# Moving part of a feed-forward stage between the attention batches of a routed kernel

## The chip, the cores and the metric

The kernel runs on one core of a Trainium2 chip. The metric is the device time of one execution in microseconds (us), as the median of several runs. The engines are named as in the profile: PE (TensorE, matmuls), PEld (its weight loads), DVE (VectorE), ACT (ScalarE), POOL (GpSimd) and SP (SyncE, which issues transfers).

## The reference, cut to what matters

```python
# q, k, v: batch 8, heads 8, sequence 576, head size 64
scores = scale * q @ k.T;  mask = |i - j| <= 32
x = softmax(scores) @ v                        # laid out as 4608 rows of 512
logits = x @ w_gate + modality_bias[modality]  # 8 experts
e_idx = argmax(logits);  gate_w = softmax(logits)[e_idx]
for e in range(8):                             # rows of expert e only
    out[mask] = gate_w * (relu(x[mask] @ w1[e]) @ w2[e])   # 512 -> 1024 -> 512
```

With the fixed inputs only two experts are used: expert 0 by 2300 rows and expert 4 by 2308.

## The kernel before

The kernel works through eight batches. Each has **attention** (transpose queries and keys, scores, Exp, mask, product with the values) and then **routing** (transpose the rows, logits, the expert of each row, the row's rank within its expert, and a scatter of the rows to a scratch in HBM, grouped by expert). When all batches are done it makes a table of 256-row tiles on the chip and runs the **feed-forward** tile by tile. PSUM is the memory into which PE writes here, and which DVE or ACT then read. Each stage has its own PSUM buffers, since a stage's pools are closed before the next stage opens its own. "tag" and "bufs" say which tiles share a buffer and how many there are.

```python
# attention and routing
ps_s bufs=1, ps_o bufs=1, ps_t bufs=2                # PSUM pools of this stage
for b in range(B):
    ...
    for hp in range(H // 2):                         # a pair of heads
        for u in range(2):
            tp = ps_t.tile([P, R, P], BF16, tag="tp")
            ...                                      # 4 transposes, then a copy to qkT
        sA = ps_s.tile([P, 2, 512], FP32, tag="sA")  # two score buffers
        sB = ps_s.tile([P, 2, 512], FP32, tag="sB")
        ...
        oA = ps_o.tile([P, 3, 2, D + 1], FP32, tag="oA")
        oB = ps_o.tile([P, 2, 2, D + 1], FP32, tag="oB")
        ...
    lg = ps_o.tile([P, NM, E], FP32, tag="oB")       # logits: an output buffer
    for m in range(NM):
        tp = ps_t.tile([P, n_kd, P], BF16, tag="tp")
        ...                                          # transpose, copy, 4 matmuls into lg
    ...
    rk = ps_o.tile([P, NM + 1, E], FP32, tag="oA")   # ranks: an output buffer
    ...                                              # 5 scatters to scr
# feed-forward, with pools of its own
fps_t bufs=2, fps_h bufs=3, fps_y bufs=3
def ffn(tiles, pools, first_block):
    ...
    for x_ in range(n):
        i = tiles[x_]
        if x_ + 1 < n:
            stage_load(tiles[x_ + 1])                # fetched and transposed a tile ahead
        up(i)                                        # 32 matmuls, Relu on ACT
        if x_:
            down(tiles[x_ - 1])                      # 16 matmuls, gate on DVE, scatter on POOL
    down(tiles[-1])
```

The softmax here doesn't subtract the row's maximum and nothing guards it: scores larger than these inputs give would overflow.

Of the kernel before, what the change touches and what calls it, by code (L numbers as in the profile page):

```python
# [31 lines left out]
def kernel(  # L32
# [28 lines left out]
    NTILE = N // TT + E - 1  # L61
    NK = N // TT
    BIG = 65536.0
    n_kd = HD // P
# [4 lines left out]
    wpool = ctx.enter_context(tc.tile_pool(name="wpool", bufs=1))  # L69
    small = ctx.enter_context(tc.tile_pool(name="small", bufs=2))  # L70

    scr = dram.tile([E * N, ROW // 2], I32)


    ident = const.tile([P, P], BF16)
    make_identity(nc, ident[:])

# [6 lines left out]
    nc.gpsimd.memset(mask[:], 1.0)  # L84
    for j in range(2):
# [6 lines left out]
    nc.gpsimd.memset(maskl[:], 1.0)  # L92
    m_ap = maskl[:]
    nc.gpsimd.affine_select(out=m_ap, in_=m_ap, compare_op=ALU.is_ge, fill=0.0,
                            base=64, pattern=[[1, 96]], channel_multiplier=-1)
    nc.gpsimd.affine_select(out=m_ap, in_=m_ap, compare_op=ALU.is_ge, fill=0.0,
                            base=0, pattern=[[-1, 96]], channel_multiplier=1)
    nc.gpsimd.affine_select(out=m_ap, in_=m_ap, compare_op=ALU.is_ge, fill=0.0,
                            base=-64, pattern=[[0, 96]], channel_multiplier=1)
# [8 lines left out]
    def iota_f(shape, pattern, base, cm):  # L108
        n = 1
        for s_ in shape[1:]:  # L110
            n *= s_
        ti = const.tile([P, n], I32, name=f"ioi{iota_f.c}")
        tf = const.tile([P, n], FP32, name=f"iof{iota_f.c}")
        iota_f.c += 1
        nc.gpsimd.iota(ti[:], pattern=pattern, base=base, channel_multiplier=cm)
        nc.vector.tensor_copy(tf[:], ti[:])
        return ti, tf
    iota_f.c = 0
    ids_i, _ = iota_f([P, B, NM], [[S, B], [P, NM]], -32, 1)
    _, io_e8 = iota_f([P, E], [[1, E]], -E, 0)  # L120
    _, io_row = iota_f([P, E], [[N, E]], 0, 0)
    _, io_k = iota_f([P, NK], [[TT, NK]], 0, 0)
    _, io_p2 = iota_f([P, 2], [[P, 2]], 0, 1)
    _, io_t = iota_f([P, NTILE], [[1, NTILE]], 0, 0)

# [4 lines left out]
    le = const.tile([P, E, E], FP32)  # L130
    nc.gpsimd.memset(le[:], 1.0)
    nc.gpsimd.affine_select(out=le[:], in_=le[:], compare_op=ALU.is_ge, fill=0.0,
                            base=0, pattern=[[1, E], [-1, E]], channel_multiplier=0)

    sgn = const.tile([P, NTILE + 1], FP32)
    nc.gpsimd.memset(sgn[:], 0.0)
    nc.gpsimd.memset(sgn[:].rearrange("p (n two) -> p n two", two=2)[:, :, 0:1], 1.0)
    off = const.tile([P, NTILE + 1], FP32)
    off_i = const.tile([P, NTILE + 1], I32)
    nh = (NTILE + 1) // 2  # L140
    nc.gpsimd.iota(off_i[:, 0:nh], pattern=[[-1, nh]], base=-1, channel_multiplier=0)
    nc.gpsimd.iota(off_i[:, nh:2 * nh], pattern=[[1, nh]], base=0, channel_multiplier=0)
    nc.vector.tensor_copy(off[:].rearrange("p (n two) -> p two n", two=2),
                          off_i[:].rearrange("p (two n) -> p two n", two=2))
# [4 lines left out]
    nc.scalar.dma_start(mb_bc[:], moe_modality_bias.partition_broadcast(P))  # L149
# [4 lines left out]
    for m in range(NM):  # L154
        p0 = 32 if m == 0 else 0
        p1 = 96 if m == NM - 1 else P
        s0 = P * m - 32
        nc.scalar.dma_start(mid64[B * m:B * m + B, p0:p1], idv[:, s0 + p0:s0 + p1])
# [4 lines left out]
    with (tc.tile_pool(name="setup", bufs=1) as sup,  # L163
          tc.tile_pool(name="setup_ps", bufs=1, space=bass.MemoryType.PSUM) as sup_ps):
        midp = sup_ps.tile([P, NM * B], BF16)
        nc.tensor.transpose(midp[:], midr[:], ident[0:NM * B, 0:NM * B])
        msel = sup.tile([P, NM * B], FP32)
        mtmp = sup.tile([P, NM * B, E], FP32)
        for m_ in range(n_mod):
            nc.vector.tensor_scalar(out=msel[:], in0=midp[:], scalar1=float(m_), scalar2=None,  # L170
                                    op0=ALU.is_equal)
            dst = bias if m_ == 0 else mtmp
            nc.vector.tensor_tensor(
                out=dst[:], in0=msel[:].unsqueeze(2).to_broadcast([P, NM * B, E]),
                in1=mb_bc[:, m_, :].unsqueeze(1).to_broadcast([P, NM * B, E]), op=ALU.mult)
            if m_:
                nc.vector.tensor_tensor(out=bias[:], in0=bias[:], in1=mtmp[:], op=ALU.add)
    bias_v = bias[:].rearrange("p (m b) e -> p m b e", b=B)

    w1_sb = [wpool.tile([P, n_kd, F], BF16, name=f"w1_{i}") for i in range(2)]  # L180
    w2_sb = [wpool.tile([P, n_kf, HD], BF16, name=f"w2_{i}") for i in range(2)]
# [10 lines left out]
    def reg(ap, engines, lo, hi):  # L192
        return nc.values_load(ap, engines=engines, min_val=lo, max_val=hi,
                              skip_runtime_bounds_check_because="the table is clamped on chip")



    qk_t = [const.tile([P, H // 2, 2, 32 + S], BF16, name=f"qkT{i}") for i in range(2)]
    p_t = [const.tile([P, 2, PW], BF16, name=f"pt{i}") for i in range(3)]
    v_t = [const.tile([P, NM, H, D + 1], BF16, name=f"vt{i}") for i in range(2)]  # L200
    x_t = [const.tile([P, NM, ROW // 2], I32, name=f"xt{i}") for i in range(2)]
    for t_ in x_t:
        nc.gpsimd.memset(t_[:, :, HD // 2 + 2:ROW // 2], 0)
    for t_ in qk_t:
        nc.gpsimd.memset(t_[:, :, 0, 0:32], 0.0)
    for t_ in p_t:
        nc.gpsimd.memset(t_[:, :, 0:4 * SW].rearrange("p h (j c) -> p h j c", c=SW)[:, :, :, WIN:SW], 0.0)
        nc.gpsimd.memset(t_[:, :, 4 * SW + WL:PW], 1.0)
    for t_ in v_t:
        nc.gpsimd.memset(t_[:, :, :, D:D + 1], 1.0)  # L210
        nc.gpsimd.memset(t_[0:P - SR, NM - 1, :, 0:D], 0.0)

    zero = const.tile([P, TT // P, ROW // 2], I32)
    nc.gpsimd.memset(zero[:], 0)

    zero_ins, scr_ins = [], []

    def after(ins, others):
        for o_ in others:
            tc.add_manual_dep(ins.ins, o_.ins.name, mybir.DependencyInfo(  # L220
                mybir.DependencyClass.Sync, mybir.DependencyReason.DATA), reason="scratch rows")

    def unordered(ins, group):

        tc.declare_no_dep(ins.ins, group=group, reason="disjoint rows")
        tc.add_to_no_dep_group(group, ins.ins)

    base = const.tile([P, E], FP32)
    ext_e = const.tile([P, NTILE + 2], FP32)
    nc.gpsimd.memset(base[:], 0.0)  # L230

    with (
        tc.tile_pool(name="ld", bufs=3) as ld,
        tc.tile_pool(name="ldv", bufs=4) as ldv,
        tc.tile_pool(name="ldr", bufs=2) as ldr,
        tc.tile_pool(name="ldb", bufs=3) as ldb,
        tc.tile_pool(name="rt", bufs=2) as rt,
        tc.tile_pool(name="ps_s", bufs=1, space=bass.MemoryType.PSUM) as ps_s,
        tc.tile_pool(name="ps_o", bufs=1, space=bass.MemoryType.PSUM) as ps_o,
        tc.tile_pool(name="ps_t", bufs=2, space=bass.MemoryType.PSUM) as ps_t,  # L240
    ):
        for b in range(B):

            cb = [[None, None], [None, None]]
            rf = ldr.tile([SR, 2, H, D], FP32, tag="rf")
            nc.sync.dma_start(rf[:, 0], q[b, :, SM:S, :].rearrange("h s d -> s h d"))
            nc.sync.dma_start(rf[:, 1], k[b, :, SM:S, :].rearrange("h s d -> s h d"))
            rb = ldr.tile([SR, 2, H * D], BF16, tag="rb")
            nc.gpsimd.tensor_copy(rb[:], rf[:].rearrange("p u h d -> p u (h d)"))
            for g in range(2):  # L250
                for u, src in ((0, q), (1, k)):
                    f_ = ld.tile([P, 4, R * D], FP32, tag="qkf")
                    nc.sync.dma_start(
                        f_[:], src[b, 4 * g:4 * g + 4, 0:SM, :].rearrange("h (p r) d -> p h (r d)", r=R))
                    c_ = ldb.tile([P, R, 4 * D], BF16, tag=f"cb{u}")
                    o_ap = c_[:].rearrange("p r (h d) -> p h r d", h=4)
                    i_ap = f_[:].rearrange("p h (r d) -> p h r d", r=R)
                    if u == 0:
                        nc.gpsimd.tensor_copy(o_ap, i_ap)
                    else:  # L260
                        nc.scalar.copy(o_ap, i_ap)
                    cb[u][g] = c_
# [358 lines left out]
```

## Time and profile before

| | before |
|---|---|
| median time | 416.99 us (415.33 to 418.84, 3 runs) |
| end of routing of the last batch (its rank matmul) | 247.6 us |
| a steady batch, mean of the last five | 24.9 us |
| from the last rank to the end | 169 us, of it 130 us of full PE |
| mean granted PE clock, as recorded (1 is full speed) | 0.73 |

The prediction below quotes the busy tenths, the windows and the chain of waits. One more stretch is the PE timeline around a head pair's scores (start us, duration us, then what was run):

```profile
199.20 0.50 PE L309 MATMUL sA<-qkT 64*128 64x192 bf16 x4
199.50 0.60 PE L309 MATMUL sB<-qkT 64*128 64x192 bf16 x6
```

The second half of the scores starts 0.30 us after the first, into the second buffer, without waiting for the Exp of the first half.

### The profile page before, as it was taken

How to read it: one execution, taken by the hardware profiler on the slowest of the kernel's cores; microseconds unless marked ns; L12 is line 12 of the kernel's file. 1: busy time of each engine (PE TensorE's matmuls, PEld its weight loads, DVE VectorE, ACT ScalarE, POOL GpSimd, SP SyncE). 2: the span in 40 equal slices, each digit the busy share in tenths (PEclk: the TensorE clock that was granted, in tenths of full speed). 3: DMA queues.
4: the chain of work that ended last, by engine and by line, in shares of the span. 5: the costliest groups of instructions: out<-in, count | busy, mean ns of one | idle time of the engine just before them, and what ended most of it. 6: DMA issues, size and time to landing. Idle time of an engine off the chain costs nothing. (4 is left out here: it accounts for less than half of the span.)

```text
span 416.7 us, 7245 instructions
## 1 busy us (share of the span) xinstructions
PE 280.7 (67%) x2649; PEld 197.0 (47%) x2649; DVE 212.2 (51%) x569; ACT 157.8 (38%) x229; POOL 141.1 (34%) x235
## 2 busy tenths in 40 slices
PE   0017766650365766657667740999999999999960
PEld 0015544440254544535445530867677676776720
DVE  1626897740576886868878674223232232323220
ACT  0038584443036376381744610423324233242400
POOL 9632366103546153452420404023122131222230
PEclk9999655555555555565555555899999999999995
DMA  9999979996593834846100103113323242332220
GB/s 122 236 315 306 257 187 245 222 238 145 166 182 116 200 91 151 173 142 153 38 37 2 62 0 110 58 29 128 106 103 131 79 129 104 104 129 80 101 105 1
DMA packets 79080, 55.06 MB, mean 132 GB/s; under 512 B 49176, under 2 KB 74560, under 8 KB 79040
## 3 DMA queue, kind: packets, MB, share of 16 engines
q1 hardware_dynamic: 32688, 26.40, 22.6%
q0 software_dynamic: 8624, 18.66, 15.1%
q10 hardware_dynamic: 37728, 9.49, 12.3%
q8 instruction: 23, 0.38, 0.4%
q14 instruction: 17, 0.14, 0.1%
HBM read 121.75 MB, written 17.76 MB: 335 GB/s over the span
## 5 line engine op out<-in xcount | busy, mean ns | idle before, releaser
L537 ACT ACTIVATE hT<-ph 128x512 bf16<-128x512 f32 x76 | 45.4, 597 | 103.8 <-PE ph L535 103.3
L535 PE MATMUL ph<-xT,w 128*128 128x256 bf16 x608 | 70.1, 274 | 0.0
L549 PE MATMUL py<-w,hT 128*128 128x512 bf16 x304 | 68.6, 379 | 0.0
L554 POOL DMA_INDIRECT out_dram<-ys,ix x38 | 36.8, 969 | 87.1 <-DVE ys L552 73.6
L535 PEld LDWEIGHTS <-w 128*128 128x128 bf16 x608 | 59.1, 98 | 7.0
L298 ACT COPY qkT<-tp 128x512 bf16<-128x512 bf16 x32 | 41.3, 1317 | 48.6 <-PE tp L293 20.5
L404 POOL DMA_INDIRECT scr<-xt,di x40 | 39.9, 997 | 52.9 <-DVE pt L321 16.2
L330 PEld LDWEIGHTS <-pt 128*128 128x128 bf16 x320 | 28.9, 123 | 49.7 <-DVE pt L315 31.1
L296 DVE COPY qkT<-tp 128x512 bf16<-128x512 bf16 x32 | 41.4, 1295 | 20.1 <-PE tp L293 19.2
L330 PE MATMUL oA<-vt,pt 128*128 128x65 bf16 x192 | 25.2, 238 | 33.8 <-DVE pt L315 21.8
L552 DVE TENSOR_SCALAR ys<-py,xg 128x512 f32<-128x512 f32 x38 | 28.4, 751 | 38.2 <-PE py L549 38.2
L549 PEld LDWEIGHTS <-hT 128*128 128x128 bf16 x304 | 29.8, 98 | 32.0
L315 DVE TENSOR_TENSOR pt<-pt,mask 128x768 bf16<-128x768 bf16 x64 | 37.9, 607 | 2.1 <-ACT pt L313 2.0
L313 ACT ACTIVATE pt<-sB 128x768 bf16<-128x768 f32 x32 | 25.9, 810 | 32.9 <-PE sB L309 29.2
L544 DVE TENSOR_TENSOR ix<-xg,pen_i 128x2 int32<-128x2 int32 x19 | 3.0, 160 | 62.1 <-DMA out_dram<-ys,ix 57.4
L313 ACT ACTIVATE pt<-sA 128x768 bf16<-128x768 f32 x32 | 26.3, 821 | 13.9 <-PE sA L309 9.1
L351 PE MATMUL tp<-ident,xt 128*128 128x128 bf16 x160 | 26.6, 299 | 5.7 <-DVE xt L341 3.3
L335 PEld LDWEIGHTS <-pt 128*128 128x128 bf16 x256 | 28.5, 129 | 0.0
L309 PEld LDWEIGHTS <-qkT 64*128 64x128 bf16 x320 | 16.7, 118 | 19.1 <-ACT qkT L298 8.0
L309 PE MATMUL sA<-qkT 64*128 64x192 bf16 x128 | 16.8, 340 | 10.6 <-ACT pt L313 5.2
L309 PE MATMUL sB<-qkT 64*128 64x192 bf16 (+1 forms) x192 | 22.6, 323 | 0.1
L335 PE MATMUL oA<-vt,pt 128*128 128x65 bf16 x128 | 22.2, 241 | 0.0
(265 smaller groups left out, 404.5 us busy)
## 6 DMA issues: line engine op xcount, KB each, us to landing
w<-in_moe_w_dram POOLq DMA_DIRECT2D x42, 1024.0 KB
xg<-scr SPq DMA_DIRECT2D x19, 272.0 KB, 2.8
scr<-zero SPq DMA_DIRECT2D x8, 272.0 KB, 3.0
rf<-in_q_dram SPq DMA_DIRECT2D x8, 128.0 KB, 4.5
rf<-in_k_dram SPq DMA_DIRECT2D x8, 128.0 KB, 7.3
scr<-xt,di POOLq DMA_INDIRECT x40, 2.5
out_dram<-ys,ix POOLq DMA_INDIRECT x38, 2.7
f__219<-in_q_dram SPq DMA_DIRECT2D x1, 512.0 KB
```

What stands on the lines that cost most here:

```text
L296: nc.vector.tensor_copy(o_ap, tp[:])
L298: nc.scalar.copy(o_ap, tp[:])
L309: nc.tensor.matmul(s_t[:, h, c0:c0 + w_], kT[D * h:D * h + D, k0:k0 + P], qT[D * h:D * h + D, q0:q0 + w_], start=True, stop=True)
L313: nc.scalar.activation(p_ap, s_t[:, :, 0:2 * WIN].rearrange("p h (j c) -> p h j c", c=WIN), ACT.Exp, scale=scale)
L315: nc.vector.tensor_tensor(out=p_ap, in0=p_ap, in1=mask[:].unsqueeze(1).to_broadcast([P, 2, 2, WIN]), op=ALU.mult)
L330: nc.tensor.matmul(o_t[:, m - m0, h, :], pt[:, h, SW * m:SW * m + P], vt[:, m, 2 * hp + h, :], start=(m == m0 and h == 0), stop=(m == 0), ...
L335: nc.tensor.matmul(o_t[:, m - m0, h, :], pt[:, h, c1:c1 + P], vt[:, m - 1, 2 * hp + h, :], start=False, stop=True, skip_group_check=True)
L404: ins = nc.gpsimd.indirect_dma_start(out=scr[:], out_offset=bass.IndirectOffsetOnAxis(ap=di[:, m:m + 1], axis=0), in_=xi[:, m, :], in_offs ...
L535: nc.tensor.matmul(ph[:, u, :], w1[:, kd, P * mi:P * mi + P], xTs[i][:, kd, :], start=(kd == 0), stop=(kd == n_kd - 1))
L537: nc.scalar.activation(hT[:, 2 * mp:2 * mp + 2, :], ph[:], ACT.Relu)
L549: nc.tensor.matmul(py[:], hTs[i][:, kf, P * s:P * s + P], w2[:, kf, :], start=(kf == 0), stop=(kf == n_kf - 1))
L554: ins = nc.gpsimd.indirect_dma_start(out=out, out_offset=bass.IndirectOffsetOnAxis(ap=ix[:, s:s + 1], axis=0), in_=ys[:], in_offset=None, ...
```

## The change

In the feed-forward PE is busy for 130.0 of 130 us, in attention for 26.6 of 40 (windows in the prediction), so the change puts the two beside each other. After each batch's routing, up to one full 256-row tile of the first and of the last used expert is fetched and run: 14 tiles in all. Five tiles are left for a tail from the table. The stages now run at once, out of one set of PSUM pools, with fewer buffers for each. Loads and set-up are also reordered at the start.

```diff
-    (pools of one stage, closed before the next one's are opened)
+    ps_s bufs=1, ps_o bufs=1, ps_t bufs=2, ps_h bufs=1, ps_y bufs=1    # all at once
 ...
-                sA = ps_s.tile([P, 2, 512], FP32, tag="sA")
-                sB = ps_s.tile([P, 2, 512], FP32, tag="sB")
+            for j0 in (0, 2):
+                st = ps_s.tile([P, 2, 512], FP32, tag="s", name="st")
 ...
-            lg = ps_o.tile([P, NM, E], FP32, tag="oB")
+        lg = ps_t.tile([P, NM, E], FP32, tag="tp", name="lg")
-            rk = ps_o.tile([P, NM + 1, E], FP32, tag="oA")
+        rk = ps_t.tile([P, NM + 1, E], FP32, tag="tp", name="rk")
 ...
+    route(0)
+    choose()                       # first and last used expert; load their weights
+    slots = dispatch()             # the next full tile of each, or an empty one
+    for b in range(1, B):
+        Cb = cast(b, L1)
+        if b + 1 < B:
+            L1 = load(b + 1)
+        attend(b, *Cb)
+        route(b)
+        nxt = dispatch() if b + 1 < B else None
+        for t in slots:
+            t.fetch()              # xg, transposes, xT, and ix = row ids | penalty on DVE
+            run(t)                 # 4 x (quarter of up, quarter of the previous tile's down)
+        slots = nxt
 ...
+    tail(range(N_TAIL), True)      # N_TAIL = 5
+    with tc.If(n_tiles > N_TAIL, preferred_fallthrough_block=False):
+        tail(range(N_TAIL, NTILE), False)
```

The transposed queries and keys are now written to SBUF contiguously and read from PSUM in steps, where before it was the other way round. The routing's copies move from DVE to ACT.

## The prediction

> **What bounds the kernel now.** I read the page first, for the busy tenths in 40 slices, because the change moves work from one stage into another.
>
> ```profile
> PE   0017766650365766657667740999999999999960
> DVE  1626897740576886868878674223232232323220
> PEclk9999655555555555565555555899999999999995
> DMA  9999979996593834846100103113323242332220
> ```
>
> A slice is 10.4 us. Slices 3 to 23 are attention and routing: the TensorE (PE) is half to three quarters busy at half clock and the VectorE (DVE) is the fullest engine. Slices 25 to 38 are the feed-forward: the PE is full at full clock while everything else idles. So there are two regimes, one after the other, with different limits. The DMA is full for the first 100 us only.
>
> Next I cut the span into windows (length, then busy us of PE, weight load, DVE, ACT, POOL; granted clock; DMA share; GB/s).
>
> ```profile
> 140.00:180.00 40.00, 26.59 (x312) 19.77 (x310) 31.47 (x91) 19.50 (x26) 16.52 (x21) 0.50 0.63 153
> 180.00:220.00 40.00, 26.74 (x317) 19.13 (x314) 30.06 (x84) 21.25 (x31) 14.52 (x17) 0.54 0.32 88
> 245.00:262.00 17.00, 2.27 (x29) 1.80 (x26) 10.09 (x51) 0.24 (x1) 5.05 (x9) 0.50 0.30 95
> 262.00:392.00 130.00, 130.00 (x989) 91.14 (x987) 37.96 (x68) 42.99 (x72) 32.33 (x66) 0.99 0.28 95
> 392.00:417.00 25.00, 10.61 (x65) 6.17 (x63) 3.75 (x5) 2.39 (x4) 5.36 (x7) 0.80 0.17 65
> ```
>
> In steady attention DVE is 75 to 79% busy and nothing is saturated. The 17 us from 245 to 262 are a bridge: last routing, table, scatter and first fetch, with PE idle. Then come 130 us of pure PE, and an end.
>
> The chain of waits shows the period of the feed-forward (start us, us, what):
>
> ```profile
> 258.05 3.33 DMA xg<-scr
> ...
> 266.52 0.45 PE tp L512 x8
> 266.96 3.49 PE ph L535 x32
> 270.46 3.45 PE py L549 x16
> 273.91 0.45 PE tp L512 x8
> ```
>
> One 256-row tile costs 0.45 + 3.49 + 3.45 = 7.39 us of PE. Running the reference's routing on its fixed inputs gives 2300 rows for expert 0, 2308 for expert 4 and none for the others, so 9 + 10 = 19 tiles, or 140 us.
>
> Last, from the timeline, I took the start of each batch's rank matmul (end of its routing): 54.8, 79.8, 123.0, 150.1, 175.8, 201.6, 225.2, 247.6. The steady batch takes 24.9 us (247.6 minus 123.0, over five). The third batch took 43.2 us: the two experts' weights were issued at 64.5 to 67.9, DMA was full until about 108, and one DVE write waited 17.7 us for a scatter queued behind them.
>
> [...] 0.50 through attention, and in two-us windows 0.50 at 260 to 262, 0.63 at 262 to 264, 1.00 after, with the feed-forward's start. [...]
>
> ```profile
> L298 ACT COPY qkT<-tp 128x512 bf16<-128x512 bf16 x32 | 41.3, 1317 | 48.6 <-PE tp L293 20.5
> L296 DVE COPY qkT<-tp 128x512 bf16<-128x512 bf16 x32 | 41.4, 1295 | 20.1 <-PE tp L293 19.2
> L353 DVE COPY xT<-tp 128x512 bf16<-128x512 bf16 x40 | 16.2, 421 | 6.9 <-PE tp L351 6.0
> ```
>
> Same size and types, but L296 and L298 write 2 bytes every 8 and take three times L353's time.
>
> **The change, part by part.**
>
> *Start.* The first q and k loads move ahead of everything; eight zero fills of 272 KB shrink to one at this point, and POOL set-up moves behind batch 0 or to DVE. Before, the first q load was issued only at 18.2 us, after the zero fills, and the first transposes ran at 25.5. I expect them at about 8 us, so the first rank at 36 instead of 54.8, and weights issued at about 46 instead of 64.5.
>
> *Weights.* They still share the DMA with two batches' inputs. Taking the same 43 us from issue to a free DMA gives 89 us. The first two feed-forward tiles need them, so batch 2 finishes some 17 us later: rank of batch 2 at 106 instead of 123.
>
> *Tiles moved.* From the reference's routing, the cumulative rows of expert 0 after each batch are 288, 591, 877, 1173, 1467, 1753, 2021 and of expert 4 288, 561, 851, 1131, 1413, 1703, 2011. Each time both exceed the next multiple of 256, so all 14 slots hold a real tile: 14 x 7.39 = 103 us of PE leaves the serial stage. Left are 508 and 516 rows: 2 + 3 = 5 tiles, exactly the unconditional tail.
>
> *What a batch then costs.* DVE per batch now: 31.47/40 x 25.7 = 20.2 us. Remove 5 x 0.42 = 2.1 (routing copies go to ACT) and about 2.6 if the four transposed copies, now written contiguously, drop from 1.30 to 0.65 (a guess between the two rows above). Add two tiles at 0.68 + 0.16 + 2 x 0.75 = 2.3 each, 4.7, and nine small dispatch operations at 0.19, 1.7: about 22 us. ACT: 19.50/40 x 25.7 = 12.5, minus 2.6, plus 8 x 0.60 = 4.8, plus about 2.5: 17. POOL: 10.6, plus four output scatters at 1.28 spacing, 5.1: 16. PE: 17.1 us busy at half clock plus 14.8 at full clock is 32; if the tiles keep the clock up part of the time, attention's share shrinks towards 9 to 12, so 24 to 32. PE and DVE share the bound [...]. The instruction order is not program order (transposes of the next batch ran at 221.6 while the rank matmul before them waited until 225.2), so ready tiles can fill PE holes. Against it: score tiles have one PSUM buffer instead of two, up and down outputs one each instead of three, and lg and rk now take transposing buffers. I take 31.5 us per batch. Five batches: 106 + 158 = 264.
>
> *After the last rank.* Before: 12.4 us from 247.6 to the first fetched tile. After: the same chain plus eight end fills, each with a register read; but the last two slots (14.8 us of PE) lie beside it. I take 16 us, to 280.
>
> *Tail.* 5 tiles at 7.7 (7.39 plus a little for the transposing copy, no longer prefetched a tile ahead), then the last half tile, 3.5: 322. Before, the last matmuls ended at 402.6 and the span at 416.7, a fixed 14 us. Sum: 336 us.
>
> As a balance: 417 - 17 (start) + 5 x 6.6 = 33 (longer batches) - 97 (169 us after the last rank become 72) = 336.
>
> **The rivals.**
>
> *Serial tiles.* If in-order queues make the tiles stand between batches instead of inside them, a batch takes 24.9 + 14.8 = about 40, and the sum is 106 + 200 + 72 = 378. For it: [...] each output scatter on POOL waits for its scaled rows ahead of the next casts. Against it: the reordering seen at 221 to 225 us.
>
> *The clock stays at half.* Then PE would need 17.1 + 2 x 14.8 = 47 us per batch, and the time would be about 415, no gain. For it: attention at 66% PE busy never raised the clock. Against it: dense tiles raised it within some 2 us, and a tile is 7 us of dense matmuls.
>
> *Single PSUM buffers bind.* Scores, Exp of half A, scores, Exp of half B then run in turn: 0.5 + 0.8 + 0.6 + 1.15 plus hand-overs of about 0.1 each, 3.5 us per head pair, against 4.6 now. So that alone does not bind attention; for the up stage an eviction of 0.6 lies beside 0.86 of down matmuls. Worth perhaps 2 us a batch, up to 350 in all.
>
> *Strided PSUM reads are no cheaper.* The copies now read PSUM at 256-byte steps; nothing in the trace shows such a read. Without the gain DVE is at 25 us, the batch about 34: 349.
>
> *Everything packs.* A batch of 27 gives 314.
>
> **Range and chances.** The batch time carries the range: 27 to 38 us over five batches moves the result by 55 us; the start and bridge add some 10. I predict 336, from 312 to 368. Slower by over 2% would need the half clock and a failed start together; I give 0.04, within 2% 0.03, faster 0.93.
>
> **What would show it.** Right: first transposes before 10 us; steady ranks 29 to 34 apart; feed-forward matmuls between attention matmuls with the clock mostly above 0.8; last rank near 264; five tiles of 7.4 to 8 after a bridge filled by matmuls; some 14 us at the end. Wrong: ranks 38 or more apart with PE idle while DVE or POOL wait for each other; clock 0.5 in the mixed stage; L296's successor still at 1.3 us; a PE hole of over 10 us at the weights (after 60 us) or before the tail.

The sum: 106 + 158 + 16 + 42 + 14 = 336 us. That interleaving the two stages gains, and that a batch of 24 to 32 us of PE work takes 31.5, were estimates of mine and not shown. The figures that begin with "0.50 through attention" are granted PE clocks. A wait that is in the trace: DVE's small write at 108.28 us had waited 17.68 us for a scatter, and DVE ran nothing meanwhile. The hand-overs of "about 0.1" are 0.04 to 0.31 us in the trace of before: 0.04 from PE's transposes to ACT's copy at 202.39, 0.12 from ACT's copy to PE's weight load at 199.20, 0.31 from the first half of the scores to its Exp at 200.01.

## The result, and the profile after

The changed kernel is correct and **slower**: 444.1 us median (443.01 to 445.83, 4 runs) against 416.77 us (415.33 to 418.84, 4 runs) of the kernel before in the same rounds. The ratio is 1.0655, 95% interval 1.0598 to 1.0713. Ratios here are the mean time of one kernel's fast runs over that of the other's of the same rounds, so they are not quite the ratio of the quoted medians. The prediction was 336 us.

The busy tenths of after, in 40 slices of 11.1 us:

```profile
PE   0445371459674967496749674967497748999920
DVE  2277271422383338323822382338233825232210
PEclk9999999999895889588958895889588956999975
DMA  9999979993374237422741250121012107411120
```

The two regimes of before are now a pattern with a period of four slices. PE goes 9, 6, 7, 4. The 9 is tiles, the 4 is routing with the clock near half (0.52 in the last window below). DVE peaks (8) beside the 7, in attention. The stages mostly take turns.

The start of each batch's rank matmul, which ends its routing, gives the account:

| us | 1 | 2 | 3 | 4 | 5 | 6 | 7 | 8 | end |
|---|---|---|---|---|---|---|---|---|---|
| before | 54.8 | 79.8 | 123.0 | 150.1 | 175.8 | 201.6 | 225.2 | 247.6 | 416.7 |
| after | 55.1 | 97.3 | 142.7 | 187.0 | 231.5 | 276.0 | 320.4 | 363.9 | 442.8 |
| predicted | 36 | | 106 | | | | | 264 | 336 |

After the last rank the kernel became 90 us shorter (169.1 to 78.9), but the last rank comes 116 us later (247.6 to 363.9). A steady batch takes (363.88 - 142.70) / 5 = 44.2 us, not 31.5.

One steady batch of after, cut in windows (length, then busy us of PE, PEld, DVE, ACT and POOL with their counts, granted clock, DMA share, GB/s):

```profile
231.50:244.20 12.70, 12.54 (x103) 8.97 (x105) 3.89 (x19) 4.42 (x8) 6.15 (x7) 0.82 0.22 72
244.20:254.00 9.80, 6.64 (x43) 3.76 (x43) 3.46 (x7) 3.06 (x7) 2.72 (x3) 0.83 0.20 66
254.00:266.50 12.50, 8.87 (x124) 5.46 (x125) 10.68 (x23) 8.36 (x14) 4.07 (x6) 1.00 0.54 183
266.50:276.00 9.50, 3.47 (x39) 2.15 (x40) 2.19 (x11) 3.16 (x6) 2.38 (x5) 0.52 0.07 16
```

In the first window PE is full, 11.1 of its 12.5 us with tiles, and DVE does 3.9 us of work in 12.7. In the third, attention, DVE is 85% busy. In the fourth, routing, no engine is busy half the time. Each window has its own limit, as before the change. Tile products run from 231.64 to 261.17 us; beside the routing there is none.

Inside the second window PE stands still for 3.0 us in the middle of a tile. The timeline of several engines, put in order of time:

```profile
241.97 1.33 SPq L420 DMA_DIRECT2D xg<-scr  x2
...
242.77 0.34 PE L228 MATMUL st<-qkT 64*128 64x192 bf16 x3
243.09 1.03 PE L444 MATMUL ph<-xTf,w 128*128 128x256 bf16 x8
...
244.93 0.16 DVE L434 TENSOR_TENSOR ix<-xg,pi 128x2 int32<-128x2 int32 x1 [7.87 <-DMA xg<-scr]
...
246.26 0.16 DVE L434 TENSOR_TENSOR ix<-xg,pi 128x2 int32<-128x2 int32 x1 [0.70 <-DMA xg<-scr]
246.34 0.74 DVE L457 TENSOR_SCALAR ys<-py,xg 128x512 f32<-128x512 f32 x1
...
247.13 0.58 PE L453 MATMUL py<-w,hT 128*128 128x512 bf16 x1 [3.01 <-DVE ys L457]
...
252.00 0.29 PE L228 MATMUL st<-qkT 64*128 64x192 bf16 x3
```

PE waits for `ys`, which frees the one output buffer of the tiles. `ys` stands in DVE's queue behind two `ix` operations of 0.16 us each, and those wait for the rows of the *next* batch's tiles, whose fetch was issued only after this batch's five scatters. DVE does nothing for 7.87 us.

The kernel's text has the tiles in one block, but the build moved the first transposes and scores of the next batch in among them (`st` between the `ph` above). PE then kept to the built order: of the six score matmuls of one group three run at 242.77, and the other three, into the same buffer and from the same operand tile, only at 252.00, behind the tile's products, while PE stands still for 3.0 us.

The scores of one head pair in after (x4, then x6, with the last group of the pair before), to be set beside the two lines of before:

```profile
260.46 0.38 PE L228 MATMUL st<-qkT 64*128 64x192 bf16 x6
261.97 0.34 PE L228 MATMUL st<-qkT 64*128 64x192 bf16 x4 [0.18 <-ACT pt L239]
263.42 0.38 PE L228 MATMUL st<-qkT 64*128 64x192 bf16 x6
```

Score groups are now 1.5 us apart, in step with ACT's Exp, which has to empty the single buffer before the next group may be written. Here are the routing's matmuls:

```profile
268.18 0.27 PE L346 MATMUL lg<-wg_sb,xTr 128*128 128x8 bf16 x4 [0.73 <-ACT xTr L344]
268.31 0.59 PE L342 MATMUL tpx<-ident,xt 128*128 128x128 bf16 x4
269.63 0.27 PE L346 MATMUL lg<-wg_sb,xTr 128*128 128x8 bf16 x4 [0.73 <-ACT xTr L344]
```

The logits `lg` hold one of the two transposing buffers for the whole routing. So transpose, copy (0.58) and logits run strictly in turn, 1.45 us a step, five steps.

Some expected things did come out. The groups of the copies out of PSUM (line, engine, tile, count, busy us, mean ns, idle before):

```profile
L216 DVE COPY qkT<-tp 128x512 bf16<-128x512 bf16 x32 | 21.9, 686 | 6.4 <-PE tp L212 5.8
L218 ACT COPY qkT<-tp 128x512 bf16<-128x512 bf16 x32 | 18.8, 590 | 5.6 <-PE tp L212 5.1
L344 ACT COPY xTr<-tpx 128x512 bf16<-128x512 bf16 x40 | 23.4, 585 | 50.5 <-PE tpx L342 46.5 <-DMA rf<-in_k_dram 2.3 <-DMA qkf<-in_k_dram 0.9
```

Reading PSUM in steps and writing SBUF contiguously costs 0.69 us on DVE and 0.59 on ACT, where the opposite cost 1.30 and 1.32. Copies of the same size that do both contiguously take 0.42 us on DVE (L353 in the prediction) and 0.59 on ACT (L344 above). So the stepped read cost nothing on ACT and 0.27 us on DVE. And the tail, on the PE timeline:

```profile
404.43 0.61 PE L428 MATMUL tpf<-ident,xg 128*128 128x128 bf16 x8
412.13 0.61 PE L428 MATMUL tpf<-ident,xg 128*128 128x128 bf16 x8
```

A tail tile takes 7.70 us, as predicted.

### The profile page after: what moved, and what is told of

It is laid out like the page before. It is cut to its first block, busy times and chain, and to the rows that moved or that the text cites. A ratio compares the mean times of both kernels' runs of the same rounds, so it can differ in the third digit from the quotient of the medians.

```text
span 442.8 us, 7035 instructions
## 1 busy us (share of the span) xinstructions
PE 284.5 (64%) x2618; PEld 184.3 (42%) x2649; DVE 183.8 (42%) x528; ACT 161.1 (36%) x269; POOL 140.5 (32%) x206
## 5 line engine op out<-in xcount | busy, mean ns | idle before, releaser
L444 PE MATMUL ph<-xTf,w 128*128 128x256 bf16 x608 | 89.8, 297 | 1.9 <-ACT hT L446 1.4
L232 ACT ACTIVATE pt<-st 128x768 bf16<-128x768 f32 x64 | 51.9, 811 | 39.3 <-PE st L228 35.7
L247 PE MATMUL ot<-vt,pt 128*128 128x65 bf16 x320 | 31.1, 208 | 31.8 <-DVE xt L258 15.3
L234 DVE TENSOR_TENSOR pt<-pt,mask 128x768 bf16<-128x768 bf16 x64 | 41.8, 656 | 18.5 <-ACT pt L232 18.4
L107 POOL TENSOR_SCALAR vt<-vf 128x512 bf16<-128x512 f32 (+1 forms) x40 | 25.2, 645 | 57.1 <-DMA vf<-in_v_dram 30.9
L344 ACT COPY xTr<-tpx 128x512 bf16<-128x512 bf16 x40 | 23.4, 585 | 50.5 <-PE tpx L342 46.5
L247 PEld LDWEIGHTS <-pt 128*128 128x128 bf16 x320 | 22.3, 104 | 46.7 <-DVE pt L234 25.9
L228 PE MATMUL st<-qkT 64*128 64x192 bf16 (+1 forms) x320 | 29.3, 263 | 10.4 <-ACT pt L239 5.4
L342 PE MATMUL tpx<-ident,xt 128*128 128x128 bf16 x160 | 26.8, 292 | 10.7 <-DVE xt L258 10.7
L212 PE MATMUL tp<-ident,cb 128*128 128x128 bf16 x256 | 28.0, 247 | 5.3 <-DVE qkT L216 3.8
L252 PE MATMUL ot<-vt,pt 128*128 128x65 bf16 x256 | 29.5, 206 | 0.0
L258 DVE TENSOR_TENSOR xt<-ot,rec 128x640 bf16<-128x640 f32 x32 | 26.3, 823 | 1.0
```

Source lines behind the costliest of these rows:

```text
L212: nc.tensor.transpose(tp[:, i, :], C[u][g][:, i, D * l:D * l + P], ident[:])
L228: nc.tensor.matmul(st[:, h, c0:c0 + w_], kT[D * h:D * h + D, k0:k0 + P], qT[D * h:D * h + D, q0:q0 + w_], start=True, stop=True)
L232: nc.scalar.activation(p_ap, st[:, :, 0:2 * WIN].rearrange("p h (j c) -> p h j c", c=WIN), ACT.Exp, scale=scale)
L234: nc.vector.tensor_tensor(out=p_ap, in0=p_ap, in1=mask[:].unsqueeze(1).to_broadcast([P, 2, 2, WIN]), op=ALU.mult)
L247: nc.tensor.matmul(o_ap, pt[:, h, SW * m:SW * m + P], vt[:, m, 2 * hp + h, :], start=(m == 0), stop=(m == 0), skip_group_check=True)
L342: nc.tensor.transpose(tp[:, kd, :], xr[:, m, P * kd:P * kd + P], ident[:])
```

## The experiments

The theory after reading the trace had two parts. **In series**: the tiles stand in in-order queues ahead of most of a batch's own work, so that they add nearly their whole PE time to it, and small operations that wait for a transfer stand ahead of the ones PE waits for. **Buffers**: attention itself became slower because it lost PSUM buffers. The rivals were that DVE or PE is simply full, that the added transfers slow the loads, or that the age of the tile lists is what matters. "Batch" below is always the mean of the last five ranks; it was 24.9 us before and 44.2 after. All kernels were timed in three rounds against the kernel before. In the rounds of the experiments (chip 2 of the machine, run 13 on chip 15) the kernel before took 421.3 to 422.4 us, against 416.8 in the rounds of the result, whose chip the record doesn't name, so times are to be compared as ratios. The changed kernel itself was timed in the rounds of the result only, so where a run is compared with it I go by the batches of the traces.

**1. Without the index operation at the fetch (correct).** The scatter takes its row ids straight from the fetched rows, and rows of the zero page carry an id out of range.

```diff
-            nc.vector.tensor_tensor(out=self.ix[:]..., in0=xg[:, :, HD//2+1:HD//2+2],
-                                    in1=self.pen_ap..., op=ALU.bitwise_or)
+    nc.gpsimd.memset(zero[:, :, HD // 2 + 1:HD // 2 + 2], 1 << 30)
-                 ap=self.ix[:, s:s + 1]
+                 ap=self.xg[:, s, HD // 2 + 1:HD // 2 + 2]
```

> The 128x2 index operation of each tile is gone (the padding rows carry an out-of-range index instead). Theory that this operation, hoisted ahead of the output scaling in the VectorE queue, makes the 3.0 us TensorE hole of each steady batch: rank-to-rank time 44.4 falls to about 41, the time from 444 to about 423, and the scaling of the first tile no longer waits behind a fetch. Rival (the tiles stand in series anyway and the hole is refilled by another wait): under 5 us gained.

Measured: 428.81 us, ratio 1.0158 (1.0138 to 1.0177). The batch is 42.0 us. The operation of 0.16 us cost 2.3 us a batch, and the profiled span fell from 442.8 to 426.9 us. The blocked queue is real, but it is the smaller part of the 19 us by which a batch grew.

**2. Logits and ranks out of the transposing buffers (correct).**

```diff
-        lg = ps_t.tile([P, NM, E], FP32, tag="tp", name="lg")
+        lg = ps_o.tile([P, NM, E], FP32, tag="o", name="lg")
-        rk = ps_t.tile([P, NM + 1, E], FP32, tag="tp", name="rk")
+        rk = ps_s.tile([P, NM + 1, E], FP32, tag="s", name="rk")
```

> The logits and the rank matmul leave the transposing buffers (lg goes to the output bank, rk to the score bank), so the five routing transposes get two buffers. Theory that the serial transpose, copy, logits loop (1.45 us a step) is due to the shared buffers: routing stretch of 9.5 us falls to about 7, time 444 to about 425. Rival (the copy on ScalarE and the hand-overs set the step): under 5 us gained.

Measured: 414.38 us, ratio 0.9803 (0.9773 to 0.9834). The batch is 40.0 us. Two names changed, nothing of the work, and 4.2 us a batch came back. This alone undoes the loss.

**3. The tiles spread (correct).** The two tiles are cut into eight chunks (a quarter of up and a quarter of down). One is placed after each head pair and after each of the first four routing steps. The lists are those of two batches ago, so that the fetch never waits for scatters just issued.

```diff
+            if hook is not None:
+                hook(hp)          # in attend, after each head pair; the same in route
-        for t in slots:
-            t.fetch()
-            run(t)
+            ta, tb = queue.pop(0); ta.fetch()      # b >= 2; tb after the third head pair
+            attend(b, *Cb, hk[0]); route(b, hk[1]) # hooks: one chunk each
+        queue.append(dispatch())
```

> Nothing removed; the eight chunks of the two tiles are placed one after each head pair and one after each routing step, from the lists of two batches ago, instead of in a block between batches. Theory that the place of the tiles in the queues is the cause: steady rank-to-rank time about 33 instead of 44.4, time about 362. Rival (single PSUM buffers and engine contention make any mixture slow): rank-to-rank stays at 40 or more, time 420 or more.

Measured: 389.39 us, ratio 0.9226 (0.9208 to 0.9244). The batch is 34.1 us, ten less than after.

**4. All three together (correct).**

> The three edits before together. Order theory: rank-to-rank about 28, time about 332, faster than both kernels. Rival: above 400.

Measured: 374.18 us, ratio 0.8846 (0.8798 to 0.8893). The batch is 33.4 us. This beats both kernels by a wide margin. Some PE lines of it:

```profile
239.79 1.06 PE L446 MATMUL ph<-xTf,w 128*128 128x256 bf16 x4
240.64 0.63 PE L212 MATMUL tp<-ident,cb 128*128 128x128 bf16 x4
241.21 0.50 PE L228 MATMUL st<-qkT 64*128 64x192 bf16 x4
241.64 0.61 PE L446 MATMUL ph<-xTf,w 128*128 128x256 bf16 x2
```

The tile's up products (`ph`) stand between transposes and scores of attention, as some did in after; here a part of them is left for every head pair and for the routing. Once the tiles fill the holes, the freed buffers of run 2 and the removed operation of run 1 are worth only 0.7 us a batch more; 8 us of the step from 389 to 374 come earlier, with the third rank at 125.5 us instead of 133.7.

**5. No tiles between the batches (correct).** All 19 tiles go to the tail, and the lists of tiles (`dispatch()`, eight small operations of DVE a batch) are not made between the batches. Everything else of the change stays.

```diff
-        for t in slots:
-            t.fetch()
-            run(t)
-    N_TAIL = 5
+    N_TAIL = 19
```

> All 19 tiles in the tail; nothing runs between the batches, the rest as in the changed kernel. Order theory: attention and routing alone take 25 us a batch in the new buffers, so the tiles stood in series with them (44.4 - 25 = 19.4 us for two tiles); last rank near 245, then a bridge of 18, 19 tiles at 7.7, 3.5 and an end of 16: about 430. Rival (the single score and output buffers made attention itself slow): 29 us or more a batch, 455 or more.

Measured: 466.1 us, ratio 1.1057 (1.0989 to 1.1126). The batch is (274.89 - 124.95) / 5 = 30.0 us, where the kernel before takes 24.9. So attention *without any tile* became 5.1 us a batch slower. Two tiles of 7.39 us on top make 44.8, and after has 44.2: in sum hardly anything was gained by overlap.

**6. Half the weights (relative error 0.73).** Its output is wrong, which doesn't matter for the time. Only one expert's weights are loaded at the start, to see if the volume of the weights is what delays the second and third batch.

```diff
-            load_w(1, i, e_r)
-            load_w(2, i, e_r)
+            if i == 1:
+                load_w(1, i, e_r)
+                load_w(2, i, e_r)
```

> Wrong result on purpose: the changed kernel without the weights of one of its two experts (zeros instead), so 4.2 MB fewer to move. Theory that the first 140 us are bound by the DMA engines and not by when the first load is issued: the rank of batch 2, now at 142.7, comes some 15 us earlier (4.2 MB at 211 to 260 GB/s are 16 to 20 us) and the time falls from 444 to about 429. Rival (the early stage is bound by queues that wait for each other): under 5 us.

Measured: 440.78 us, ratio 1.0437 (1.0366 to 1.0509). The rank of the third batch is at 138.7 instead of 142.7 us: two of the four weight transfers less moved it by 4 us, and 2 of these are there at the first rank, before any weights are loaded. The volume of the weights is not the main cause.

**7. Old lists, but in blocks (correct).** The lists of two batches ago as in run 3, with the tiles in one block after the routing as in after.

```diff
+        if b + 1 < B:
+            queue.append(dispatch())
+        if b >= 2:
+            for t in queue.pop(0):
+                t.fetch(); run(t)
```

> The changed kernel's block of two tiles after each routing, but from the lists of two batches ago, as the spread version uses. Theory that the place in the queues mattered in the spread version: this one stays near 425 to 430 (only the waits for fresh fetches go). Rival (the older lists were what helped): near 390.

Measured: 442.47 us, ratio 1.0499 (1.0476 to 1.0522). The batch is 42.3 us. The age of the lists is worth 2 us a batch; the other 8 us that run 3 gained come from the place of the tiles in the queues.

**8. All chunks within attention (correct).** As run 4, but two chunks after each head pair and none in the routing.

```diff
+            def hook_a(n):
+                for u_ in (2 * n, 2 * n + 1):
+                    chunk(ta if u_ < 4 else tb, u_ % 4)
+            hk = [hook_a, None]
```

> The version with all three edits, but all eight chunks inside attention, two per head pair, and none beside routing. If work beside the routing chain is worth its length: rank-to-rank rises from 33 to about 37 and the time from 374 to about 395. If the order of the queues evens it out: within 6 us of 374.

Measured: 373.05 us, ratio 0.8849 (0.8800 to 0.8898), the same as run 4. The batch is 32.2 us. That the tiles are spread matters; between these two ways of spreading them there is no difference in time.

**9. No tiles between, and run 2's edit (correct).**

> All 19 tiles stand in the tail (no tile work between batches), as in the run that took 29.6 us a batch where the kernel before takes 24.9; and the logits and ranks of the routing no longer take the two transposing buffers, but the output and score banks. Theory 1, the 4.7 us a batch are lost because logits and ranks share the transposing buffers: a batch falls to about 25.3 us (29.6 less the 4.3 that the same edit saved with tiles in between), and the time to some 1.045 of the kernel before (466 less 6 x 4.3 = 440 where before is 417 to 422). Theory 2, the one score bank instead of two is what slows attention: a batch stays above 28 us and the time above 1.08 of before.

Measured: 442.64 us, ratio 1.0468 (1.0428 to 1.0509). The batch falls from 30.0 to (250.37 - 118.40) / 5 = 26.4 us.

**10. The same, with two score buffers (correct).** The tiles' products take turns in the score and output buffers.

```diff
-    ps_s bufs=1;  ps_h bufs=1;  ps_y bufs=1
+    ps_s bufs=2
-            ph = ps_h.tile([P, 2, TT], FP32, tag="h", name="ph")
+            ph = ps_s.tile([P, 2, TT], FP32, tag="s", name="ph")
-                self.py = ps_y.tile([P, HD], FP32, tag="y", name="py")
+                self.py = ps_o.tile([P, HD], FP32, tag="o", name="py")
```

> As the run with all tiles in the tail and the routing's logits and ranks out of the transposing buffers, and also two score banks as in the kernel before (the feed-forward's products take turns in the score and output banks, so nothing else is short). If the shared transposing buffers are all of the 4.7 us a batch, this run has the same batch as its neighbour within 0.7 us (about 25). If the single score bank is the cause, this run alone falls to 25 us or less and its neighbour stays near 29. If each is a part, the step from the neighbour to this run is between 1 and 3 us a batch.

Measured: 437.52 us, ratio 1.0342 (1.0309 to 1.0375). The batch is 25.0 us. The 5.1 us of attention are now accounted for: 3.6 by the shared transposing buffers, 1.4 by the single score buffer, and 0.1 left, which is the net of all the other edits. The windows of the last five batches, for before, run 5, run 9 and run 10 in turn (columns as above):

```profile
123.00:247.60 124.60, 83.83 (x965) 60.04 (x965) 94.51 (x272) 64.72 (x90) 43.27 (x49) 0.51 0.38 101
```

```profile
125.00:274.90 149.90, 90.20 (x991) 60.13 (x991) 71.73 (x206) 68.91 (x117) 46.33 (x54) 0.51 0.27 79
```

```profile
118.40:250.40 132.00, 84.99 (x965) 59.27 (x964) 69.44 (x204) 67.70 (x116) 43.43 (x52) 1.00 0.31 90
```

```profile
115.60:240.50 124.90, 82.20 (x962) 57.11 (x962) 71.72 (x204) 66.36 (x116) 44.53 (x52) 0.85 0.37 104
```

PE, ACT and POOL do nearly the same work in all four, and DVE does 23 to 25 us less than before in the last three. Run 5 nevertheless needs 25 us more than before. A stage can get slower while its fullest engine is relieved by a quarter; what grew is the waits between engines. The first rank also moved, to 46.7 us.

**11. More load buffers (correct).** This tests why the first rank stayed at 55 us. A trigger of loads had been seen holding ACT's queue until a buffer was free: in after, ACT stood idle for 7.48 us before its cast at 17.88, by the profile for POOL's `vt`, which reads the loaded values; the fifth load of values, for four buffers, was issued in that time, at 16.15, after the first `vt` at 15.50.

```diff
-    ld bufs=3;  ldv bufs=4
+    ld bufs=6;  ldv bufs=10
```

> The changed kernel with more load buffers (10 for values instead of 4, 6 for queries and keys instead of 3), so that a load's trigger doesn't wait in the queue of the engine that also casts. Theory: the first rank at 55.1 instead of the predicted 36 comes from triggers that hold ACT and SP until a buffer is free; then the first rank falls to about 45 us, and the time to some 10 to 15 us below the changed kernel's (ratio to before 1.035). Rival: the DMA is full for the first 100 us, so that earlier triggers only share the same rate; then the first rank stays within 53 to 57 us and the time within 4 us of the changed kernel's (ratio 1.055 to 1.075).

Measured: 454.89 us, ratio 1.0768 (1.0741 to 1.0795). The first rank is at 54.4 us, as the rival had it, and the second at 108.3 instead of 97.3, which neither theory expected. (The trace is of the fastest of five executions, 449.1 us.) The windows of after and of this run:

```profile
60.00:100.00 40.00, 17.37 (x194) 11.74 (x192) 14.40 (x54) 13.86 (x23) 12.35 (x16) 1.00 1.02 211
```

```profile
60.00:100.00 40.00, 12.29 (x132) 7.94 (x132) 11.59 (x29) 11.24 (x19) 12.14 (x16) 1.00 1.16 237
```

The transfers move more (237 against 211 GB/s) and the engines do less. Loads of later batches, issued earlier, take their share of a full DMA from what batch 1 and the first tiles need now. That this is how the 11 us arise is my reading of the two windows; no run isolates it.

**12. The best version with more load buffers (correct).**

> The best kernel so far (tiles in eight chunks within attention, logits and ranks in their own banks, no index operation at the fetch; 0.885 of before) with the same added load buffers. If triggers bind the first two batches: rank of batch 1 falls from 95.4 to about 85, the time to 0.86 of before. If the DMA's rate binds them: ranks of the first three batches within 2 us of 52.7, 95.4 and 129.8, the time 0.88 to 0.89 of before.

Measured: 382.31 us, ratio 0.9007 (0.8953 to 0.9062): worse than run 8. Its second rank is at 100.4 us against 95.4, with a batch of 32.9. That more load buffers delay the second rank holds in another kernel; why is not isolated here either.

**13. The best version with two score buffers (correct).** Run 8 and the edit of run 10.

> The version with the tiles in chunks within attention (32.2 us a batch over the last five, 0.885 of before), and also two score banks, which the feed-forward's products share with the scores (the down products take turns with the attention's output bank). Theory 1, what slows attention alone (1.4 us a batch for the single score bank) also binds in the mixed stage: a batch falls to 30 to 31 us, the first rank from 52.7 to about 47, the time to 0.86 to 0.87 of before. Theory 2, in the mixed stage other work fills the holes that the score bank leaves, and sharing banks between the two kinds of work adds waits of its own: a batch stays at 32 us or above, and only the first rank moves (time 0.875 or above).

Measured: 389.46 us, ratio 0.9235 (0.9194 to 0.9276). The first rank is at 48.3 us instead of 52.7, but the batch is 35.8 us instead of 32.2. PE lines of a mixed stretch:

```profile
250.27 1.90 PE L453 MATMUL py<-w,hT 128*128 128x512 bf16 x8
252.34 0.83 PE L444 MATMUL ph<-xTf,w 128*128 128x256 bf16 x6
...
254.18 0.22 PE L245 MATMUL ot<-vt,pt 128*128 128x65 bf16 x2 [1.01 <-DVE ys L457]
```

The attention's output product (`ot`) waits for DVE's `ys`, because the tile's down product holds the same buffer. A buffer that helps attention alone is paid for by the tiles when both run at once. Run 8, at 0.885 of before, stays level with run 4 as the best.

## Why the prediction was wrong

The engine loads per batch came near. Over the last five batches of after the profile shows PE 157.6 / 5 = 31.5 us (predicted 24 to 32), DVE 20.1 (22), ACT 18.5 (17), POOL 13.0 (16). The balance failed elsewhere. Against 336, the trace's 442.8 is 107 us more: +19 by the first rank (55.1 for 36), +18 up to the third (87.6 us for 70), +63 in the five batches (221 for 158), +7 after the last (78.9 for 72). One of the prediction's own signs of being wrong came true: ranks 38 or more apart, with PE idle while DVE waits. And its rival of serial tiles summed to 378, outside the range of 312 to 368 that it gave.

- **"I take 31.5 us per batch" failed, +63 us.** The step assumed packing, on the ground that "ready tiles can fill PE holes". In its place PE kept to an order in which the tiles stand ahead of most of attention and none beside the routing, and the batch adds up from the runs as 24.9 + 3.6 (transposing buffers) + 1.4 (score buffer) + 14.8 (two tiles in series) = 44.7, measured 44.2. The sum closes to 0.5 us, but not every term is pure: run 1 shows 2.3 us of waiting for the `ix` operation inside it, so about 2.8 us of overlap were won elsewhere and lost again there. That the tiles cost their full 14.8 is the assumption of this sum, not a measurement; a second sum, run 9's 26.4 and two tiles, gives 41.2 where run 2 has 40.0.
- **The ground itself was misread.** The transposes that ran ahead of a waiting rank matmul in before stand ahead of it in the built program, as its listing shows: the build had placed them there, PE had not picked them. For that batch the listing has ten transposes of queries and keys, ten score products and three more transposes ahead of the rank matmul, and the trace shows the same 10, 10 and 3 from 221.58 us until the rank matmul at 225.18. The hole at 244.1 to 247.1 in after agrees: three score matmuls, alike to those at 242.77, stood behind the product for which PE waited 3.0 us. Other engines show the like: DVE's `ys` at 246.34 came behind two `ix` operations that had waited 7.87 and 0.70 us, and on POOL the scatter at 252.26 waited 3.89 us for `ys`, with the next cast behind it at 253.26. Runs 3 and 7, which differ in the place of the tiles, show that the place in the queue decides: 34.1 and 42.3 us.
- **"That alone does not bind attention" failed.** The rival of single PSUM buffers was rejected by adding durations to 3.5 us for a head pair, below the 4.6 of then. The sum covered scores and Exp, and gave no time to what the prediction itself named, that the same two transposing buffers now also carry logits and ranks. The rival was given 2 us a batch in all; runs 9 and 10 measure 5.0. The two rivals, serial tiles (40 us a batch) and single buffers, were weighed one by one and came true together.
- **Start, "the first rank at 36", failed by 19 us.** The first transposes ran at 12.8 to 13.3 us instead of 8 (they wait for POOL's cast), which is 5. From there to the rank I took 28 us from the kernel before, but it took 42. Run 10, with both buffer causes undone, puts the rank at 46.7, so some 8 of the 14 are the slower attention. The other 6 are open; more load buffers (run 11) don't recover them.
- **Second and third batch.** Without tiles this stretch takes 70.4 us in run 5, which is the 70 of the prediction (106 less 36), in which I had counted two tiles already. After took 17.2 us more. Of these 10.4 lie between the second and third rank, where the first two tiles run (14.8 us of PE). The other 6.8 lie between the first and second, where no tile product ran; run 10, without tiles, is as long there (41.9 us against 42.2), run 9 is not (36.5), and the cause is open. Half the weights (run 6) shortened the stretch from the first to the third rank by 2 us only. The reading behind "43 us to a free DMA" was also wrong: in before the DMA share falls from 1.08 (60 to 99 us) to 0.24 (99 to 108 us) at 99 us, not at 108. From 69 to 100 us POOL's casts waited 10.0, 10.2 and 7.4 us, the last two for loads of values, and the five scatters for which DVE waited 17.7 us stood behind them.
- **Right.** The guess of 0.65 us for the transposed copies holds (0.69 and 0.59). Why a write of 2 bytes every 8 takes three times as long (1.30 us for 0.42 on DVE) no run shows. PE got faster where tiles run: a 128x128 transpose of attention took 247 ns on average in after and 304 in run 5, without tiles between. (The recorded clock, 0.82 in the window of tiles, is no proof: eight 128x128 transposes in a row took 1.01 us in run 9, at 196.97, and 0.62 us in after, at 255.68, both at a recorded 1.00; and executions of the kernel before in one set of rounds recorded mean clocks of 0.72 to 0.99 with times of 422.0 to 424.4 us.) All 14 tiles moved and 5 were left, at 7.70 us. Somewhat short were the bridge after the last rank, 18.4 us for 16, and the end, 18.2 for 14.
- **Interleaving held, this way of doing it did not.** Run 3, which does no more than interleave, came to 0.923. The routing's steps of 1.45 us leave PE a gap of 0.73 us each while the logits hold one of two transposing buffers, and run 2, which frees that buffer, gains 4.2 us a batch. I weighed the interleaving and gave the buffer no time.

What stays open is the 33 us of the best versions: PE is busy for 133.5 of 161.2 us in run 8, so the remaining sixth is not explained by one wait, and the one buffer I tried there (run 13) made it worse.

## What to carry to other kernels

Interleaving two stages needs an interleaved instruction order: here PE and DVE gained nothing from work that stood behind what they waited for (3.0 us of PE, 7.87 us of DVE, in one batch), so put the pieces of one stage between the pieces of the other and fetch early enough that nothing small waits for a transfer. When stages that had PSUM in turn must share it, time each stage alone with its reduced buffers before counting on the overlap; here that alone cost 5 of 25 us a batch, and no engine's busy time showed it. And more load buffers are not free while the DMA is full: here, at a DMA share of 1.16 and 1.17 from 60 to 100 us, they made the second batch 11 and 5 us later in two kernels, by my reading because later loads came in ahead of what was needed.
